# A 192-byte filler ahead of the large buffers, so that they begin at multiples of 512 bytes in their partition

## The chip, the cores and the metric

The kernel runs on one core of a Trainium2 chip. The metric is device time of one launch in microseconds. Launches of one kernel spread by about 1%, so kernels were timed in rounds on one chip beside the kernel before; some ran at a granted clock of 0.990 to 0.992 (a clock of 1 is full speed).

## The reference

A block-wise linear attention with decay (4 batches, 8 heads, 768 tokens, head width 64) is followed by a gated feed-forward layer on the 3072 tokens of width 512:

```python
for b in range(nb):                      # blocks of 64 tokens
    intra = (qb @ kb.T * Dmask) @ vb
    inter = (qb * lam_pow) @ kv_state
    out[:, :, sl] = intra + inter
    kv_state = lam_block * kv_state + (kb * rev_pow).T @ vb
...
h = x @ w_in                             # 512 -> 2048
g = h * np.cos(h)
return g @ w_out                         # 2048 -> 512
```

Inputs and output are float32; the kernel multiplies in bf16.

## The kernel before

The kernel handles 24 blocks of 128 tokens. Those of the start are loaded as two "spans" of two blocks each; the other 20 are loaded one by one. A planner in the program puts every instruction in order. Blocks 8 to 23 transpose q and k by DMA, the earlier ones on TensorE. What the change touches is only where the buffers lie:

```python
lam_bc = consts.tile([P, H], F32)         # small constants first:
...                                       # 32 to 2048 bytes per partition
warm = consts.tile([P, 1], F32)
nc.scalar.activation(warm, halfpi, AF.Sin)

w_in_sb = consts.tile([P, KD, D_FF], BF16)    # starts at byte 24384 = 47 * 512 + 320
w_out_sb = consts.tile([P, KF, DM], BF16)
...
def add_span_load(name, src, x, prio, deps):      # 512 KB, packets of 512 B
    live["raw", x] = work.tile([P, 3, H, 2, D], F32, tag="g", name="sp_f")
    ...
    start(nc.sync, t.rearrange("u h s d -> u h (s d)"),
          src[x, :, 0:2 * P, :].rearrange("h (u s) d -> u h (s d)", s=2), deps)
...
def add_load(n, name, src, prio, deps=()):        # 256 KB, packets of 256 B
    ...
    t = loads.tile([P, H, D], F32, tag=name, name=name)
    start(nc.sync, t, src[b, :, c * P:(c + 1) * P, :].transpose([1, 0, 2]), deps)
```

Every tile from w_in_sb on has a size that is a multiple of 512 bytes, so all of them begin 320 bytes past a multiple of 512 in their partition. I call this number the remainder.

## Time and profile before

| | kernel before |
|---|---|
| launch, median | 214.95 us (214.09 to 215.8, 4 runs) |
| span in the profile | 213.1 us, clock 1.000 |
| TensorE busy | 200.6 us, 94% |
| first feed-forward matmul | 18.28 us |
| DMA full | slices 1 to 26 of 40, about 140 us |

TensorE is the engine that sets the end, while the DMA engines are full for two thirds of the time. To read such a profile, one has to find where TensorE waits for DMA; only there can a faster transfer win anything. The prediction shows the lines.

### The profile page before, as it was taken

The numbers are of one execution on the slowest core, as the hardware profiler recorded it, in microseconds if no ns is written. First come the engines' busy times: TensorE is split into PE (matmuls) and PEld (weight loads), VectorE is DVE, ScalarE is ACT, GpSimd is POOL, SyncE is SP. The second block draws the span as 40 slices with busy tenths as digits, with TensorE's granted clock in tenths as the row PEclk, the third lists the DMA queues.
The fourth block names the chain that finished last, engine by engine and source line by source line (L and its number), as shares of the span: only waits on it lengthen the run. The fifth ranks groups of instructions, "written<-read, shape, count | busy, mean of one in ns | idle before, by whom it ended". The sixth has DMA issues, their size and how long they took to land.

```text
span 213.1 us, 4584 instructions
## 1 busy us (share of the span) xinstructions
PE 200.6 (94%) x1815; PEld 117.4 (55%) x1839; DVE 122.3 (57%) x220; ACT 111.7 (52%) x206; POOL 64.7 (30%) x81
## 2 busy tenths in 40 slices
PE   6577999999998999999999999999999999999994
PEld 6355644546875766666675545545445444444453
DVE  2489676365987685565967676946643333344000
ACT  5776785313773555665655565635445554554120
POOL 4587000267613554372527445430000000000000
PEclk9999999999999999999999999999999999999999
DMA  5999999999969999999999999971001101110112
GB/s 133 290 246 206 205 206 214 222 222 231 225 139 238 163 258 177 263 217 189 235 203 237 217 216 215 220 164 52 22 27 52 49 2 49 49 52 27 72 49 98
DMA packets 93589, 33.85 MB, mean 159 GB/s; under 512 B 80128, under 2 KB 90624, under 8 KB 93568
## 3 DMA queue, kind: packets, MB, share of 16 engines
q1 hardware_dynamic: 89200, 29.24, 66.8%
q0 software_dynamic: 4224, 4.19, 12.0%
q8 instruction: 14, 0.23, 0.5%
q10 hardware_dynamic: 144, 0.13, 0.2%
q14 instruction: 7, 0.06, 0.1%
HBM read 27.27 MB, written 6.29 MB: 157 GB/s over the span
## 4 chain that ended last, share of the span: by engine, by line
PE 81%; DMA 10%; SPq 3%; DVE 2%; issue 1%; ACT 1%; ACTq 0%
PE ps_f L617 38%; PE ps_h L577 35%; DMA qkT<-qk 4%; DMA sp_f<-in_k_dram 3%; DMA w_in_sb<-in_moe_w_in_dram 3%; PE ps_s L373 3%; PE ps_o L413 2%; PE ps_o L417 2%; SPq L254 1%; DVE g L589 1%; PE ps_kv L401 1%; DVE s_m L379 1%; SPq L636 1%; PE ps_t L340 1%; SPq L346 1%
## 5 line engine op out<-in xcount | busy, mean ns | idle before, releaser
L583 ACT ACTIVATE cos<-ps_h,halfpi 128x256 f32<-128x256 f32 (+1 forms) x132 | 72.9, 571 | 63.0 <-PE ps_h L577 61.8
L589 DVE TENSOR_TENSOR g<-ps_h,cos 128x256 bf16<-128x256 f32 (+1 forms) x132 | 70.3, 544 | 54.7 <-ACT cos L583 54.1
L577 PE MATMUL ps_h<-xT,w_in_sb 128*128 128x256 bf16 (+1 forms) x523 | 95.0, 320 | 1.7 <-DMA w_in_sb<-in_moe_w_in_dram 1.2
L617 PE MATMUL ps_f<-w_out_sb,g 128*128 128x512 bf16 (+1 forms) x385 | 93.3, 370 | 1.0 <-issue 0.3
L577 PEld LDWEIGHTS <-w_in_sb 128*128 128x128 bf16 x528 | 51.0, 98 | 38.7 <-DMA w_in_sb<-in_moe_w_in_dram 1.7
L617 PEld LDWEIGHTS <-g 128*128 128x128 bf16 x400 | 38.3, 98 | 36.6
L312 POOL TENSOR_TENSOR qk<-q_f,q_scale 128x512 bf16<-128x512 f32 x19 | 20.1, 1058 | 50.7 <-DMA q_f<-in_q_dram 36.6
L629 ACT COPY o_sb<-ps_f 128x512 f32<-128x512 f32 (+1 forms) x24 | 13.8, 576 | 27.1 <-PE ps_f L617 27.1
L379 DVE TENSOR_TENSOR s_m<-ps_s,mask 128x512 bf16<-128x512 f32 x40 | 25.9, 683 | 0.7 <-PE ps_s L373 0.4
L320 POOL TENSOR_TENSOR v_s<-v_f,v_scale 128x512 bf16<-128x512 f32 x19 | 19.6, 1042 | 11.1 <-DMA v_f<-in_v_dram 8.8
L406 DVE CAST kv_bd<-ps_kv 64x512 bf16<-64x512 f32 x16 | 11.0, 688 | 4.7 <-PE ps_kv L401 4.5
L316 POOL CAST qk<-k_f 128x512 bf16<-128x512 f32 x18 | 11.0, 611 | 8.6 <-DMA k_f<-in_k_dram 8.4
L424 ACT CAST xT<-ps_o 128x512 bf16<-128x512 f32 x20 | 10.7, 588 | 1.7 <-PE ps_o L417 1.1
L692 PE MATMUL ps_idle<-blank,ident 128*128 128x128 bf16 (+1 forms) x51 | 7.3, 305 | 2.0 <-POOL ident masks.py:199 1.6
L373 PE MATMUL ps_s<-qkT 64*128 64x128 bf16 x160 | 7.3, 218 | 1.2 <-DMA qkT<-qk 1.1
L417 PE MATMUL ps_o<-s_m,v_s 128*64 128x128 bf16 x160 | 7.6, 219 | 0.0
L343 DVE COPY qkT<-ps_t 128x512 bf16<-128x512 bf16 (+1 forms) x6 | 3.1, 514 | 7.1 <-PE ps_t L340 7.1
L413 PE MATMUL ps_o<-qkT,kv_bd 128*64 128x128 bf16 x144 | 7.1, 220 | 0.0
L629 DVE COPY o_sb<-ps_f 128x256 f32<-128x256 f32 x1 | 0.4, 426 | 10.8 <-PE ps_f L617 10.8
L373 PEld LDWEIGHTS <-qkT 64*128 64x128 bf16 x160 | 4.6, 94 | 3.5 <-DMA qkT<-qk 1.7
L692 PEld LDWEIGHTS <-ident 128*128 128x128 bf16 x55 | 4.9, 126 | 2.1 <-POOL ident masks.py:199 1.6
L417 PEld LDWEIGHTS <-v_s 128*64 128x64 bf16 x160 | 5.5, 110 | 0.0
(61 smaller groups left out, 76.8 us busy)
## 6 DMA issues: line engine op xcount, KB each, us to landing
q_f<-in_q_dram SPq DMA_DIRECT2D x20, 256.0 KB, 4.3
k_f<-in_k_dram SPq DMA_DIRECT2D x20, 256.0 KB, 5.2
v_f<-in_v_dram SPq DMA_DIRECT2D x20, 256.0 KB, 5.0
out_dram<-o_sb SPq DMA_DIRECT2D x19, 256.0 KB, 2.0
w_in_sb<-in_moe_w_in_dram POOLq DMA_DIRECT2D x4, 512.0 KB, 8.5
w_out_sb<-in_moe_w_out_dram POOLq DMA_DIRECT2D x4, 512.0 KB, 14.2
out_dram<-o_sb SPq DMA_DIRECT2D x9, 128.0 KB, 3.4
sp_f<-in_q_dram SPq DMA_DIRECT2D x2, 512.0 KB, 5.6
```

The source lines that it names most:

```text
L312: vec[e].tensor_mul(live["qk", n][:, 0], live.pop(("q_f", n)), q_scale[:, c, :].unsqueeze(2).to_broadcast([P, H, D]))
L320: vec[e].tensor_mul(live["v_s", n], live.pop(("v_f", n)), v_scale[:, c, :].unsqueeze(2).to_broadcast([P, H, D]))
L373: nc.tensor.matmul(live["s", n][i][:, p, :], lhsT=live["qkT", n][h, 1, p, :], rhs=live["qkT", n][h, 0, p, :], start=True, stop=True)
L379: nc.vector.tensor_mul(live["s_m", n][:, i], live["s", n][i], mask.unsqueeze(1).to_broadcast([P, NP, P]))
L413: nc.tensor.matmul(o[h, p, :], lhsT=kv_bd[(slot - 1) % NK][:, s, p, h], rhs=live["qkT", n][:, 0, p, :], start=(p == 0), stop=False, skip_g ...
L417: nc.tensor.matmul(o[h, p, :], lhsT=live["v_s", n][:, 2 * p + i, :], rhs=live["s_m", n][:, i, p, :], start=(p == 0 and c == 0), stop=True, ...
L577: nc.tensor.matmul(t[:, :n], lhsT=w_in_sb[:, kd, f * P:(f + 1) * P], rhs=live["xT", i][:, kd, at], start=(kd == 0), stop=(kd == KD - 1))
L583: nc.scalar.activation(c[:, :n], live["h", i, f, at.start][:, :n], AF.Sin, bias=halfpi)
L589: nc.vector.tensor_mul(live["g", i][:, f, at], live.pop(("h", i, f, at.start))[:, :n], live.pop(("c", i, f, at.start))[:, :n])
L617: nc.tensor.matmul(live["f", i, j, piece][:, :width], lhsT=live["g", i][:, f, j * P:(j + 1) * P], rhs=w_out_sb[:, f, part], start=(f == 0) ...
L629: (nc.scalar.copy if eng == "ACT" else nc.vector.tensor_copy)(o[:, :width], live["f", i, j, piece][:, :width])
L692: nc.tensor.matmul(idle_ps[:, :cols], lhsT=ident, rhs=blank[:, :cols], start=True, stop=True)
```

## The change

The intent is that all load buffers begin at multiples of 512 bytes, so that their transfers may be quicker:

```diff
     warm = consts.tile([P, 1], F32)
     nc.scalar.activation(warm, halfpi, AF.Sin)
 
+
+    spare = consts.tile([P, 48], F32)
+    nc.vector.memset(spare, 0.0)
     w_in_sb = consts.tile([P, KD, D_FF], BF16)
```

## The prediction

> **What bounds the kernel now.** I read the cores view first (one core, 213.1 us, clock 1.000, so no throttle enters the comparison), then the engine shares and the forty slices, then the chain that ended last in order of time, then the busy time by stage, and last the packets of the trace. The launch took 214.87 us, median of three (214.09 to 215.8); the profiled span is 1.8 us shorter.
>
> From the page, the engine shares, the slices and the main DMA queue:
> ```profile
> PE 200.6 (94%) x1815; PEld 117.4 (55%) x1839; DVE 122.3 (57%) x220; ACT 111.7 (52%) x206; POOL 64.7 (30%) x81
> ...
> PE   6577999999998999999999999999999999999994
> ...
> PEclk9999999999999999999999999999999999999999
> DMA  5999999999969999999999999971001101110112
> ...
> q1 hardware_dynamic: 89200, 29.24, 66.8%
> ```
> Two things are full at once. TensorE (PE) is full from slice 4 to the end. The DMA engines are full from slice 1 to slice 26 (about 140 us) and nearly empty after. So the end is set by TensorE, and DMA counts only where TensorE waits for it: at the start and in a few places in the middle.
>
> The chain in order of time, its first 20 us:
> ```profile
> 2.35 1.52 SPq L254
> ...
> 3.92 7.16 DMA sp_f<-in_k_dram
> ...
> 11.38 6.78 DMA w_in_sb<-in_moe_w_in_dram
> ...
> 18.28 1.03 PE ps_h L577 x8
> ```
> The reader is to see that nearly everything up to 18.28 us is transfers: the four loads of q and k of the first two spans are complete at 11.07 us, which releases the first weight load, which lands at 18.16 us and releases the first matmul of the feed-forward part.
>
> Busy time by stage (columns: PE, PEld, DVE, ACT, POOL with counts, clock, DMA share, GB/s):
> ```profile
> 0.00:18.28 18.28, 11.77 (x214) 8.88 (x217) 10.79 (x20) 11.84 (x23) 12.42 (x23) 1.00 0.98 221
> 60.00:80.00 20.00, 18.59 (x191) 12.94 (x193) 15.07 (x33) 11.13 (x26) 7.76 (x9) 1.00 1.13 200
> 80.00:140.00 60.00, 59.56 (x580) 36.23 (x586) 41.85 (x78) 34.69 (x66) 28.66 (x34) 1.00 1.16 215
> 150.00:200.00 50.00, 49.74 (x255) 22.95 (x259) 19.99 (x30) 24.01 (x37) 0.00 (x0) 1.00 0.10 38
> ```
> TensorE's idle time is 6.5 us before 18.28 us, 1.4 us between 60 and 80 us, and 0.4 us between 80 and 140 us, while DMA is as full there (1.16; over 1 means packets overlap on an engine) as anywhere. From 150 us on there are no loads at all and the TensorE is just as dense. So a faster transfer can win time only before 80 us.
>
> The longest waits of TensorE's matmuls:
> ```profile
> PE ps_t L475 <- DVE q_sp L464: 1.6, 2, 0.9
> ...
> PE ps_h L577 <- DMA w_in_sb<-in_moe_w_in_dram: 1.2, 1, 1.2
> PE ps_s L373 <- DMA qkT<-qk: 1.1, 2, 0.8
> ```
> The third is the only wait for a transfer after the start: scores that wait for the DMA transposes of blocks 8 to 11, at 66 and 75 us.
>
> **What the packets say.** Each q, k or v load of a block moves 256 KB as 1024 packets of 256 B (64 floats of one head of one token); the loads of the first two spans pair two tokens and move 512 B each. In the trace the commonest duration is 18 ns for 256 B, 27 ns for 512 B, 84 ns for 2048 B (the output stores after 150 us) and 98 ns for a weight packet (1024 B written as bf16 from 2048 B of float32). The first three lie on a line: 9 ns more for 256 B more, 57 ns more for 1536 B more, so some 9 ns fixed and 27 B per ns. With 16 engines 18 ns is 228 GB/s and 27 ns is 303 GB/s; the trace moves 202 to 230 GB/s through most of the middle and 291 GB/s from 5 to 10 us. The loads are thus at the pace of their packets, and half of a 256 B packet is fixed cost. If alignment changes anything, it is in these 9 ns.
>
> **What the Trainium skill says.**
> - "DMA: Bandwidth & Descriptors", Specifications: transfers under 512 B miss line rate because of a read-modify-write. The trace agrees on the rate (256/18 = 14 B per ns against 2048/84 = 24), but it shows one fixed cost per packet and no step at 512 B. The rule is about size; the change leaves every size.
> - The same page, "How a descriptor splits into AXI transactions": a descriptor that doesn't start at a multiple of 256 B is cut at the boundary, and the bytes ahead of its start cost beats of 32 B as well. It speaks of reads. A load's SBUF side is a write, and its HBM reads begin at multiples of 256 B already, so whether this helps the loads no page states and no run so far shows. Stores and transposes read SBUF, and there it applies.
> - "SBUF — State Buffer", Specifications and "SBUF: two separate sides": engines see 16-byte lines, and DMA has ports of its own. All shifted addresses are multiples of 64 before and after, so I expect no change in TensorE, VectorE, ScalarE or GpSimd instructions. The trace of the kernel before cannot confirm that; the next one can.
>
> **The change part by part.**
> (a) Addresses. The allocation list of the program before puts w_in_sb at byte 24384 and q_f at 85824, both 320 past a multiple of 512 (64 past one of 256), and so are w_out_sb, the span buffers, qk, qkT, g and o_sb: all tiles after the filler have sizes that are multiples of 512. 192 more makes them all 0. The constants ahead of it stay.
> (b) One more VectorE memset of 128x48. The memset of 128x256 took 0.27 us and that of 128x1 0.06, so some 0.1 us (an estimate from these two). Program order puts it after the last table product:
> ```profile
> 4.30 0.20 DVE L210 TENSOR_TENSOR expo<-pos,lnl 128x48 f32<-128x48 f32 x1
> ...
> 5.71 0.69 DVE L464 TENSOR_TENSOR q_sp<-sp_f,q_sp 128x512 bf16<-128x512 f32 x1 [1.21 <-ACT q_sp L208]
> ```
> VectorE is idle for 1.21 us there, so it costs nothing. No wait, buffer count or order changes.
> (c) Packets, if a crossing write costs two more beats as a crossing read does. Two beats of 32 B at the 27 B per ns above are 2.4 ns (an estimate). 512 B: 27 to 24.6 ns, 9%; 256 B: 18 to 15.6 ns, 13%; stores 84 to 82; weight packets, which read 2048 B, none, as their source sets the pace.
>  - Start: transfers of q and k run from about 2.35 to 11.07 us, 8.7 us x 9% = 0.8 us. Then the first weight chunk shares the engines with what is left of v for some 2.5 us: 2.5 x 9% = 0.2 us. Sum 1.0 us, all on the path.
>  - From 18 to 35 us weights are the traffic: 0.
>  - Middle: the loads from 34 to 75 us would finish 13% sooner, some 4 us of transfers; but TensorE waits only 1.1 us for transposes and about 0.3 us around them. Of this 1.0 us is to be won, and the earlier start of TensorE makes it want the transposes 1.0 us sooner, which the 4 us cover.
>  - After 80 us, the stores and the tail: 0 to 0.1 us.
> Full effect: 1.0 + 1.0 = 2.0 us. I give it a little under one in two, as the page's rule is for reads: expected gain 0.9 us, 214.87 - 0.9 = 213.9 us.
>
> **Rivals.**
> 1. Writes don't care. Packets stay at 18 and 27 ns and only the transposes' reads of qk gain: 214.5 to 214.9 us. For it: the same line holds for stores (SBUF reads) and loads (SBUF writes), and a write may be merged behind the engine. Against it: a 9 ns fixed cost is large, and the few 32 B packets of lam_bc, which go to a place that crosses no boundary, take 7 ns, a fixed cost of some 6.
> 2. A strong effect: the fixed cost is mostly the crossing, 512 B fall to some 20 ns (26%). Then the start gains 8.7 x 26% = 2.3 us plus 0.6 us of v, the middle its 1.4 us, and TensorE alone is the bound: 4.3 us, 210.6 us, right at 2%. The order of the instructions at the start (casts, products and transposes of the spans between the loads and the matmuls) would take some of it back.
> 3. Slower: all buffers at one residue of 512 collide more, or quicker loads crowd the transposes and stores that share their queue (the transposes land in 3.1 to 5.5 us, and the spread shows that they are sensitive). Each further us at 66 and 75 us is paid by TensorE: 215.5 to 216 us. Nothing in the profile speaks for the collision; the second is limited, as total bytes don't change.
>
> **Range and chances.** The lower end is the full effect with 0.2 us more, and 0.4 us for the spread of launches: 212.3. The upper end is no effect plus the spread of +0.6 us: 215.5. A gain over 2% needs 210.6 us or less, rival 2 in full: 4%. A loss over 2% needs 219.2 us: 2%.
>
> **What would show it.** In the profile after, the commonest packet of 256 B at 15 to 16 ns and of 512 B at 24 to 25 ns, the landing of the first k load near 10.3 us and the first feed-forward matmul near 17.3 us; the waits for qkT shorter; GpSimd's products still 1042 ns and the 512-column matmuls still 216 ns apart. If packets stay at 18 and 27 ns, rival 1 holds and the time stays. If packets fall and the first matmul doesn't move, the start isn't bound by packets, as I read it. If the times of engine instructions change, the third point of the skill is wrong for this case.

## The result, and the profile after

The changed kernel took 211.79 us (median of 4, 211.73 to 212.61) against 214.95 us: ratio 0.9862, 95% interval 0.9816 to 0.9908. Ratios here are the mean time of one kernel's runs over that of the other's of the same rounds, so they are not quite the ratio of the medians quoted. A second series of six launches on one chip gave 212.65 us (211.84 to 213.3) beside 215.44 us, ratio 0.987. The gain is thus 1.3 to 1.4%. It lies below the predicted range (212.3 to 215.5) in the first series and just inside it in the second.

The page of the changed kernel, the lines that answer to those of before:

```profile
span 210.1 us, 4585 instructions
...
PE 200.1 (95%) x1815; PEld 117.3 (56%) x1839; DVE 122.4 (58%) x221; ACT 111.5 (53%) x206; POOL 64.3 (31%) x81
...
DMA  4999999999999999999999999801101100111112
...
q1 hardware_dynamic: 89200, 29.24, 61.1%
```

The same 89200 packets and the same 29.24 MB take 61.1% of a shorter span where they took 66.8%. TensorE's busy time fell by only 0.5 us, so 2.5 of the 3.0 us of span were taken out of its waiting.

The chain in order of time, at the start (columns: start, duration, what):

```profile
16.11 0.61 DVE xT L528
...
16.85 1.03 PE ps_h L580 x8
```

The first feed-forward matmul begins at 16.85 us, 1.43 us earlier. The profile follows this chain back only to 16.11 us, so it does not show that the transfers have left the path. That matmul needs two things, the first weights and the cast xT on VectorE, and the timelines (columns: start, duration, engine, what, and in brackets the idle time before it) show both. Before:

```profile
11.38 1.68 POOL L254 DMA_DIRECT2D w_in_sb<-in_moe_w_in_dram  x2 [0.52 <-DMA sp_f<-in_k_dram]
...
17.46 0.68 DVE L525 CAST xT<-ps_o 128x512 bf16<-128x512 f32 x1
```

After:

```profile
10.24 1.68 POOL L257 DMA_DIRECT2D w_in_sb<-in_moe_w_in_dram  x2 [0.19 <-issue]
...
16.03 0.67 DVE L528 CAST xT<-ps_o 128x512 bf16<-128x512 f32 x1
```

Before, the first weights landed 6.8 us after their issue, at 18.16 us, and the cast ended at about 18.14 us: two paths ended together. After, the weights land 6.2 us after their issue, at about 16.5 us (1.7 us earlier), and the cast ends at 16.70 us (1.4 us earlier), so it is the last to end. This second path comes from the loads of v: VectorE's first product of v, which waits for the first of them, moved from 12.94 to 11.52 us, and the cast ends 5.2 us after its start in both kernels.

Busy time by stage, the changed kernel (columns as in the prediction):

```profile
6.00:10.00 4.00, 3.06 (x52) 2.04 (x57) 2.16 (x5) 3.26 (x6) 2.67 (x2) 1.00 1.15 347
60.00:80.00 20.00, 19.73 (x200) 13.67 (x201) 14.81 (x33) 11.34 (x27) 9.10 (x11) 1.00 1.13 221
80.00:140.00 60.00, 59.56 (x574) 35.61 (x579) 41.59 (x76) 34.39 (x64) 28.16 (x32) 1.00 1.01 214
```

and the kernel before between 6 and 10 us, when only the span loads run:

```profile
6.00:10.00 4.00, 2.27 (x20) 1.39 (x21) 1.99 (x5) 3.17 (x5) 2.00 (x2) 1.00 1.17 290
```

The last number is the main reading: the same loads, of packets of the same size, move 347 GB/s instead of 290. Between 60 and 80 us TensorE's idle time fell from 1.4 to 0.3 us, and its list of waits has no DMA transpose any more. From the first feed-forward matmul to the end of the last one the kernel before needs 209.97 - 18.28 = 191.69 us, the changed one 207.00 - 16.85 = 190.15 us. So the account is 1.43 us at the start and 1.54 us in the middle, together the 3.0 us of the span. Of the 1.54 us, 1.14 us are idle time between 60 and 80 us that is gone; most of the rest comes with TensorE's slightly smaller busy time, which no run explains.

The packets behind the rate, counted from the trace:

| | before | after |
|---|---|---|
| 512 B packets: commonest, its share, mean | 27 ns, 28%, 32.4 ns | 27 ns, 99%, 27.5 ns |
| 256 B packets: commonest, its share, mean | 18 ns, 65%, 22.8 ns | 18 ns, 96%, 20.4 ns |
| weight packets, mean | 98.9 ns | 99.6 ns |
| start of the last 256 B packet | 141.6 us | 134.2 us |

The commonest duration did not move at all. What went is the tail above it: before, most of the 512 B packets took 28 to 41 ns. The 77824 packets of 256 B are 61440 of the block loads and 16384 more, which is what 16 DMA transposes of 256 KB come to; their numbers here are of both together. Nor is a packet's duration the time for which it keeps its engine: at 347 GB/s each of 16 engines passes 512 B in 16 x 512 / 347 = 23.6 ns, less than the 27 ns that a packet lasts, so packets overlap (the DMA share of 1.15 in the line above says the same).

Engine instructions kept their usual times: GpSimd's product v_s takes 1043 ns in the mean (1042 before) and 512-column matmuls follow each other after 216 ns in both. The memset took 0.10 us in VectorE's idle time.

### The profile page after: what moved, and what is told of

The parts are those of the page before. It is cut to its first block, busy times and chain, and to the rows that moved or that the text cites.

```text
span 210.1 us, 4585 instructions
## 1 busy us (share of the span) xinstructions
PE 200.1 (95%) x1815; PEld 117.3 (56%) x1839; DVE 122.4 (58%) x221; ACT 111.5 (53%) x206; POOL 64.3 (31%) x81
## 3 DMA queue, kind: packets, MB, share of 16 engines
q1 hardware_dynamic: 89200, 29.24, 61.1%
## 4 chain that ended last, share of the span: by engine, by line
PE 89%; ACT 1%; issue 1%; DVE 0%; ACTq 0%
PE ps_h L580 40%; PE ps_f L620 39%; PE ps_s L376 2%; PE ps_o L420 2%; PE ps_o L416 2%; PE ps_kv L404 1%; PE ps_t L343 1%; ACT xT L427 1%; PE ps_kv L502 0%; DVE xT L528 0%; PE ps_idle L695 0%; PE ps_o L514 0%; ACT o_sb L632 0%; PE ps_o L520 0%; ACTq L632 0%
## 5 line engine op out<-in xcount | busy, mean ns | idle before, releaser
L323 POOL TENSOR_TENSOR v_s<-v_f,v_scale 128x512 bf16<-128x512 f32 x19 | 19.7, 1043 | 10.1 <-DMA v_f<-in_v_dram 8.2
```

The costliest lines, as they stand in the source:

```text
L323: vec[e].tensor_mul(live["v_s", n], live.pop(("v_f", n)), v_scale[:, c, :].unsqueeze(2).to_broadcast([P, H, D]))
```

## The experiments

My theory after the result was that a packet whose place in SBUF crosses a multiple of 256 bytes is written in more pieces and holds its DMA engine longer, and that the loads alone matter. The rivals were that the memset or the particular addresses did it, that 512 is the granule, that 128 is enough, and that stores, transposes or weights have a part. Twelve runs were made, two of them repeats, all with correct results. The times are in one table; the details follow.

| kernel | remainder of 512 | median us | before, same rounds | ratio, 95% interval | GB/s, 6 to 10 us | first feed-forward matmul |
|---|---|---|---|---|---|---|
| filler512 | 320 | 214.96 | 215.78 | 0.9971 (0.9935 to 1.0006) | 290 | 18.28 us |
| residue256 | 256 | 213.23 | 215.78 | 0.9893 (0.9855 to 0.9931) | 347 | 16.83 us |
| residue384 | 384 | 214.33 | 215.78 | 0.9951 (0.9906 to 0.9997) | 290 | 18.30 us |
| residue32 | 32 | 216.12 | 215.78 | 1.0029 (0.9988 to 1.0069) | 290 | 18.29 us |
| only_spans | 0 for sp_f, else 320 | 214.62 | 215.42 | 0.9951 (0.9912 to 0.999) | 347 | 16.80 us |
| only_loads | 0 for q_f, k_f, v_f, else 320 | 213.34 | 215.42 | 0.9906 (0.9869 to 0.9944) | 290 | 18.29 us |
| all_but_loads | 320 for these four, else 0 | 215.44 | 215.42 | 0.998 (0.994 to 1.002) | 290 | 18.32 us |
| spans_and_loads | 0 for these four, else 320 | 212.57 | 215.42 | 0.9858 (0.9823 to 0.9892) | 341 | 17.09 us |
| after_again | 0 | 212.65 | 215.44 | 0.987 (0.9836 to 0.9903) | 347 | 16.83 us |
| residue256_again | 256 | 212.46 | 215.44 | 0.987 (0.9834 to 0.9905) | 346 | 16.78 us |
| filler704 | 0 | 213.0 | 215.44 | 0.9884 (0.9848 to 0.992) | 343 | 17.05 us |
| residue192 | 192 | 214.78 | 215.44 | 0.9962 (0.9919 to 1.0004) | 290 | 18.26 us |

### Which remainder

**filler512**, the control: the same extra instruction, and a filler that leaves the remainder.

```diff
-    spare = consts.tile([P, 48], F32)
+    spare = consts.tile([P, 128], F32)
```

> The filler is 512 bytes: the same extra memset and one more tensor, but every buffer stays 320 past a multiple of 512. Alignment theory: as the kernel before, 214.5 to 215.3 us, mean of the 512 B packets near 32 ns and of the 256 B packets near 23 ns. Rival (the memset or the mere shift of all addresses did it, not the alignment): 211.5 to 212.5 us.

It measured 214.96 us, ratio 0.9971 with 1 inside the interval; 512 B packets at 32.4 ns, 256 B at 22.5, and the rate as before:

```profile
6.00:10.00 4.00, 2.27 (x20) 1.39 (x22) 1.99 (x5) 3.15 (x5) 2.00 (x2) 1.00 1.17 290
```

The memset and a shift as such do nothing that these runs can see. (This profile happens to have no long stall between 60 and 80 us, but it ran at a mean clock of 0.992, so its middle is not to be compared. It does show that a launch at remainder 320 need not have that stall.)

**residue256**

```diff
-    spare = consts.tile([P, 48], F32)
+    spare = consts.tile([P, 112], F32)
```

> A filler of 448 bytes: every buffer begins 256 past a multiple of 512. Theory A (a packet that crosses a multiple of 256 is written in two pieces): as good as the change, 211.5 to 212.3 us, 512 B packets at a mean of 27.5 ns, 256 B at 20.4 ns. Theory B (512 is the granule): 512 B packets stay near 32 ns, while 256 B packets cross nothing and are fast: the start loses its 1.4 us and the time is 213 to 213.6 us.

The packets are those of the changed kernel: 27.5 and 20.3 ns, and 347 GB/s in the stage view:

```profile
6.00:10.00 4.00, 3.46 (x50) 2.12 (x53) 2.19 (x5) 3.26 (x6) 2.73 (x2) 1.00 1.15 347
```

By packets and by the start, theory A. But the time, 213.23 us, lay in the range of theory B, and the profile has a wait for a transpose at 73 us (0.68 us from one score matmul to the next). So I ran it again beside the changed kernel, below.

**residue384**

```diff
-    spare = consts.tile([P, 48], F32)
+    spare = consts.tile([P, 16], F32)
```

> A filler of 64 bytes: every buffer begins 384 past a multiple of 512, which is a multiple of 128 but not of 256. Theory A (cut at multiples of 256): slow, 214.3 to 215.5 us, and perhaps a little worse than before, means 32 and 23 ns. Rival C (128 bytes are the granule, or 64 bytes off is special): fast, 211.5 to 212.3 us.

```profile
6.00:10.00 4.00, 2.65 (x22) 1.51 (x21) 2.00 (x5) 3.19 (x5) 2.00 (x2) 1.00 1.20 290
```

Multiples of 128 are not enough: the rate is 290 GB/s, the 512 B packets take 32.8 ns and the start is where it was. The time is slightly better than before, with an interval that ends at 0.9997; the start has no part in this.

**residue32**

```diff
-    spare = consts.tile([P, 48], F32)
+    spare = consts.tile([P, 56], F32)
```

> A filler of 224 bytes: every buffer begins 32 past a multiple of 512, the smallest offset the allocator gives. Theory A: every packet still crosses a multiple of 256, and if the count of pieces is what costs, it is as slow as before: 214.3 to 215.5 us. If the cost goes with a piece that is not a multiple of 64 bytes, it is slower than before, 216 us or more. If it goes with the bytes past the boundary, it is about halfway, 213.3 us.

**residue192**

```diff
-    spare = consts.tile([P, 48], F32)
+    spare = consts.tile([P, 96], F32)
```

> A filler of 384 bytes: all buffers 192 past a multiple of 512, so a packet has 64 bytes ahead of the boundary where the kernel before has 192. If the number of pieces sets the cost and not their sizes: 290 GB/s between 6 and 10 us as before, first feed-forward matmul at 18.3 us, 214.3 to 216 us. If short first pieces are cheap: up to 340 GB/s and 212 to 213 us.

Remainders of 32 and 192 give the same rate, so with 64 (the kernel before), 128, 192 and 32 bytes past a multiple of 256 all moving 290 GB/s, it is beginning off a multiple of 256 that costs, and not how many bytes lie on which side. (A 512 B packet crosses one such multiple even when it begins at one; off it, it crosses two.)

```profile
6.00:10.00 4.00, 2.43 (x22) 1.39 (x21) 2.00 (x5) 3.13 (x5) 2.00 (x2) 1.00 1.16 290
...
6.00:10.00 4.00, 2.32 (x22) 1.40 (x22) 2.00 (x5) 3.13 (x5) 2.00 (x2) 1.00 1.22 290
```

The first line is that of residue32, the second that of residue192. The time of residue32, 216.12 us, lies where its text expected a cost of pieces that are no multiple of 64 bytes (216 us or more). But the kernel before took 215.78 us in the same rounds, and the ratio, 1.0029, has 1 in its interval, so that is not shown. Between 192 and 32 there may be a difference in the middle (0.9962 and 1.0029 of the kernel before): residue32 has the highest mean of the 256 B packets, 23.6 ns, and waits 2.4 us for transposes in its profile. The two intervals overlap, and launches at a clock of 0.992 or less make part of it: without them the ratios are 0.997 and 1.001. I don't have an explanation that a run shows.

**after_again, residue256_again, filler704**: the changed kernel, the kernel at 256, and the remainder 0 at an address 512 bytes further on.

```diff
-    spare = consts.tile([P, 48], F32)
+    spare = consts.tile([P, 176], F32)     # filler704
```

> The changed kernel unaltered, timed beside the kernels at other multiples on one chip. If multiples of 256 are all that counts, it lies within 0.3% of residue256_again and of filler704; a launch at a full clock takes 211.7 to 212.6 us where the kernel before takes 215.

> The kernel with all buffers 256 past a multiple of 512 once more. Theory: 256 is the granule, so the same as after_again within 0.3%, and the 0.7 ms-free stall of 0.68 us at 73 us that its first profile showed is chance and not tied to the address. Rival: 512 is worth something of its own, 0.4% or more slower, with the stall at 73 us in this profile too.

> A filler of 704 bytes: all buffers at multiples of 512 again, but 512 bytes further on than in the changed kernel. Theory: same as after_again within 0.3%, 99% of the 512 B packets at 27 ns. Rival (the particular addresses, not their remainder): up to 1.4% slower.

(In the second of these texts "0.7 ms-free" is a slip of the pen; the stall of 0.68 us is meant.) The three ratios are 0.987, 0.987 and 0.9884, within 0.15% of each other. So 512 has no worth of its own that these runs can see: multiples of 256 do it, and the address beyond them makes no difference beyond the noise. The longer time of the first look at 256 was not repeated. What differs between the profiled launches is whether TensorE still waits for a transpose: residue256_again had one such gap at 64 us (0.63 us), and even the changed kernel had two in this series' profile, around 73 us (0.84 and 0.75 us), in a launch of 213.17 us. The start's gain stands in every profile with sp_f at a multiple of 256; the middle's comes and goes in part, so one profile can't show it and the timed rounds must. Such waits are likely a part of the spread of 211.7 to 213.3 us; the clock is another (the launch of 213.3 us ran at 0.992).

### Which buffers

Fillers at the head of each pool set the remainder of the pools apart; a filler after the span buffers sets back what follows them.

**only_spans**

```diff
+    pad_w = work.tile([P, 48], F32, tag="pad_w", bufs=1, name="pad_w")
     lam_bc = consts.tile([P, H], F32)
...
                 live["raw", x] = work.tile([P, 3, H, 2, D], F32, tag="g", name="sp_f")
+                if x == 1:
+                    work.tile([P, 80], F32, tag="pad_g", bufs=1, name="pad_g")
```

> Only the two span load buffers sp_f (and g, which takes their place later) begin at multiples of 512; all else stays at 320. If the start's gain comes from the 512 B loads alone: first feed-forward matmul at 16.9 us as in the changed kernel (18.3 before), 512 B packets at 27.5 ns, waits for qkT as before or longer as TensorE is earlier: 213.0 to 214.9 us. Rival (another buffer, as w_in_sb, makes the start faster): first matmul stays at 18.3 us, 214.9 us.

TensorE's timeline shows the start of the changed kernel:

```profile
16.80 1.03 PE L580 MATMUL ps_h<-xT,w_in_sb 128*128 128x256 bf16 x8 [1.23 <-DVE xT L528]
```

So the whole of the start comes from six transfers. The time fell by 0.5%, about 1.1 us (0.2 to 1.9 us by the interval), which agrees with the 1.4 us of the start. With the 256 B loads as slow as before, TensorE still waits, at 38, 64 and 74 us (0.64, 0.73 and 0.49 us from one matmul to the next). Whether a part of the gain is given back there is not shown: this profile's span, 211.7 us, is 1.4 us below that of before.

**only_loads**

```diff
+    pad_l = loads.tile([P, 48], F32, tag="pad_l", bufs=1, name="pad_l")
+    pad_t = toks.tile([P, 80], F32, tag="pad_t", bufs=1, name="pad_t")
     lam_bc = consts.tile([P, H], F32)
```

> Only q_f, k_f and v_f begin at multiples of 512. If the 256 B loads are what shortens the middle: first matmul at 18.3 us as before, the wait for qkT of 1.1 us is gone and the middle's 1.5 us are won: 213.2 to 213.7 us. Rival (the transposes, which read qk and write qkT, were the slow ones): 214.5 to 215 us.

The middle, from the stage view of this kernel:

```profile
60.00:80.00 20.00, 20.00 (x205) 14.07 (x204) 15.38 (x34) 11.77 (x27) 7.99 (x9) 1.00 1.04 206
```

TensorE is busy in all 20 us. The time fell by 0.9%, about 2.0 us (1.2 to 2.8 us by the interval), with the start at 18.29 us as before. The transposes still read qk and write qkT at 320, and they land as long after their issue as before (4.0 us in the median, 4.2 before); but the first is issued at 58.1 us, where it was 60.5 us. They were late because their inputs were late, not because they were slow.

**all_but_loads**

```diff
 (to the changed kernel)
+    pad_l = loads.tile([P, 80], F32, tag="pad_l", bufs=1, name="pad_l")
+    pad_t = toks.tile([P, 48], F32, tag="pad_t", bufs=1, name="pad_t")
+    pad_w = work.tile([P, 80], F32, tag="pad_w", bufs=1, name="pad_w")
...
+                if x == 1:
+                    work.tile([P, 48], F32, tag="pad_g", bufs=1, name="pad_g")
```

> The reverse: weights, qk, qkT, v_s, o_sb and all others begin at multiples of 512, sp_f, q_f, k_f and v_f at 320. If only writes of loads matter: 214.5 to 215.2 us. If reads by stores and transposes count, as the prediction allowed: up to 1 us faster, 213.9 us. If the other buffers did it all: 211.8 us.

```profile
6.00:10.00 4.00, 2.49 (x23) 1.39 (x21) 1.99 (x5) 3.11 (x5) 2.00 (x2) 1.00 1.17 290
```

Ratio 0.998 with 1 inside the interval: weights, transposes and stores at multiples of 512 are worth nothing that can be seen. (The store packets of 2048 B do change, 70% of them take 84 ns here and 39% before, but their mean stays at 94 ns.)

**spans_and_loads** has the edits of only_spans and only_loads together.

> sp_f, q_f, k_f and v_f at multiples of 512, all else at 320. If the load buffers are the whole of it: 211.6 to 212.2 us, as the changed kernel. If the rest counts as well: 212.4 to 213.4 us.

Ratio 0.9858, as the changed kernel's 0.9862. Its median, 212.57 us, lies in the range for "the rest counts as well", but the kernel before was slower as well in those rounds (215.42 us), so the ratio is the number to go by. The two parts add up within their intervals: 1.1 us of only_spans and 2.0 us of only_loads make 3.1, and both together took 215.42 x 0.0142 = 3.1 us off. Each of the three is known to some 0.8 us, so that they agree to the tenth is luck.

No experiment points to a version that beats the changed kernel; several equal it.

## Why the prediction was wrong, point by point

- **What bounds the kernel: right, but for one path.** Only the start and the waits before 80 us had anything to give, and the gain came from just these two places. The start moved because its six loads did (only_spans), the middle because the block loads did (only_loads). What the prediction did not see is that the first matmul waited for two things that ended together, the weights (18.16 us) and VectorE's cast (about 18.14 us), and that the cast hangs on the loads of v.
- **Part (a), (b) and the engines: right.** The memset is hidden, and engine instructions did not change.
- **"Two beats of 32 B at the 27 B per ns above are 2.4 ns" is the step that failed.** It is a term of the sum that was mis-sized, and the start's gain was worked out from it. At the sustained rate 16 engines pass a 512 B packet in 16 x 512 / 290 = 28.2 ns each before and in 16 x 512 / 347 = 23.6 ns after, a difference of 4.6 ns, nearly twice mine. A packet was to take 9% less time; it took 16% less (the rate rose by 347/290, 20%). Instead of 1.0 us the start gave 1.43 us: the first weights are issued 1.14 us earlier where I had 0.8, they land another 0.5 us sooner where I had 0.2, and of these 1.7 us VectorE's cast, which now ends 0.2 us after the weights, lets 1.43 through. And the cost does not follow bytes ahead of a boundary, as my beats would have it: 32, 64, 128 and 192 bytes all give 290 GB/s.
- **The commonest duration was the wrong quantity to read.** I took 27 and 18 ns as what the packets cost, drew a line through them and looked for the misalignment in its fixed 9 ns. But these durations are the same at every remainder, in all fourteen profiles. Nor do they give the pace: I turned 27 ns into 303 GB/s and, with 291 measured, took the loads to be at the pace of their packets, while the changed kernel moves 347 GB/s with packets that still last 27 ns, as they overlap. The misalignment sat in the spread that I passed over: only 28% of the 512 B packets of before took 27 ns, and their mean was 32.4 ns. A mean and a share of the commonest value, or the bytes per time in a stretch with only these packets, would have shown that there was more to win. My test "if packets stay at 18 and 27 ns, rival 1 holds and the time stays" was wrong for the same reason: they stayed, and the time fell.
- **The middle's 1.0 us: the mechanism right, the size low.** It gave 1.54 us in the first profile. I counted the wait for transposes and a little around it; the kernel with no such wait (only_loads) won 2.0 us. That the quicker loads cover what the earlier TensorE wants is borne out: the first transpose is issued at 56.5 us where it was 60.5 us.
- **Halving the effect for doubt** took off another 1.1 us. I gave the full effect a little under one in two because the page's rule is for reads. These writes, too, are slower off a multiple of 256, though not by the page's beats. The full effect as I had sized it, 2.0 us, would still have missed the 3.0 us of the profiles. (214.87 - 0.9 is 213.97, so the expected time should have read 214.0 us.)
- **Rivals.** Rival 1 (writes don't care) falls, except that what it granted to the transposes' reads is not there either: all_but_loads gains nothing measurable. Of the rivals, rival 2 (a strong effect, up to 4.3 us) was nearest, but too strong: a packet lost 16% and not 26%. At the start the order of the instructions took some of the gain back, as it said: VectorE's cast ends 0.2 us after the first weights have landed. Rival 3 did not happen.

What stays open is why it costs as much as it does. The runs show that packets that begin off a multiple of 256 on the SBUF side are slow, at all four offsets tried; that the packet is cut into more pieces there is argued from the page and not shown. Nor was it tried whether the target's own alignment counts or its difference from that of the source in HBM, whose pieces lie at multiples of 256 in their tensor.

## What to carry to other kernels

Where a kernel has thousands of packets of 256 or 512 bytes into SBUF, look up the addresses of their buffers: a small tensor ahead of them can leave them all off a multiple of 256, and a filler of a few bytes repairs it. When judging packets in a trace, read the bytes per time in a stretch where only they run, which the overlap of packets does not mislead; the mean and the spread show a delay that the commonest duration hides. And before expecting time from it, check where the bound engine waits for these transfers; here 20% on the rate was 1.3 to 1.4% on the time.

## What the Trainium skill lacked or had wrong

- "DMA: Bandwidth & Descriptors", How a descriptor splits into AXI transactions: it tells of reads that begin off a multiple of 256 B. Writes into SBUF are slower as well, and not by the beats it counts: 512 B packets went at 290 GB/s alike at 32, 64, 128 and 192 bytes past a multiple of 256, and at 341 to 347 GB/s at 0.
- The same page, Specifications, names 512 B as the least size for line rate and says nothing of alignment; at one size the rate differed by 20%.
- "SBUF — State Buffer", Operand start alignment: it gives what is legal and says that its runs timed nothing. In this kernel engine instructions kept their usual times (1042 and 1043 ns for a GpSimd product) while DMA into the same buffers did not.
- No page says that a misaligned packet keeps its usual duration (27 ns) and shows only in the spread (a mean of 32.4 ns against 27.5 ns).
